# A drain between the halves of a chunk's turning, and low parts by a product with minus one, in a fused RWKV and gated-convolution kernel

## The chip, the cores and the metric

The kernel runs on one core of a Trainium2 chip. Its metric is device time in microseconds (us) of one execution. Three timed runs of the kernel before gave 322.41, 322.68 and 322.76 us; the median is 322.68 us.

## The reference, cut to what matters

All inputs are 32-bit, apart from the three weights of the second part, which are 64-bit floating point. The first part is a recurrence over 768 steps for 4 batches of 8 heads of 48 channels, the second a projection, a convolution over three neighbours in time, a gate and a projection back:

```python
for t in range(S):                       # B=4, H=8, S=768, D=48
    cur = einsum('bhd,bhe->bhde', u * k[t], v[t])
    y[:, :, t] = einsum('bhd,bhde->bhe', r[t], state + cur)
    state = w[t] * state + einsum('bhd,bhe->bhde', k[t], v[t])
x = y laid out as (B, S, H*D = 384)
h = maximum(x @ w_in, 0)                 # 384 -> 1024
c = conv_w[0] * h[t-1] + conv_w[1] * h[t] + conv_w[2] * h[t+1]
out = (h * sigmoid(c)) @ w_out           # 1024 -> 384
```

## The kernel before, in words

**Chunks.** The recurrence is cut into 24 chunks of 128 steps (4 batches of 6). For a chunk, w, k and r are loaded with time on the partitions and turned by TensorE so that channels stand on the partitions (`turns`, three banks of PSUM: w, k and r). VectorE writes zeros into four columns of w's bank (`pad`, L598), runs two scans over w (L646, L654) and multiplies k and r by them (L651, L658). The scaled keys are turned back (`kback`), scores are products of keys and r (L756, or L764 in half chunks), VectorE puts them under a mask (L796), and `within` (L848) makes the chunk's output y in one bank. The state goes from chunk to chunk through small products (L813, L878) and small vector operations.

**Turning late chunks.** The turning of chunks 0 to 7 is whole (L632, 128 by 128). From chunk 8 on (`MERGED`) it is done in two parts, f1 and f2, of 12 small transposes each (L780), in which two transposes on different halves of TensorE's rows run side by side; the keys of the chunk before are turned back in the same parts. The two halves of a row group write the same bank in f1 and in f2, with their places changed, so the end of f1 and the start of f2 must not overlap. Before, that is kept by `pad`: it waits for f1, and f2 waits for it. Between f1 and f2 the written order puts other work of TensorE.

**High and low parts.** Matrix products take numbers in a rounded 32-bit form (fp32r). A number is split into a high part and the rest, the low part, and three products (high with high, high with low, low with high) stand for one. For y, ScalarE copies the high part from the bank (L856), and VectorE subtracts it from the bank and stores the low part (L857).

**Blocks.** As soon as its chunks are there, each of 8 blocks of 384 steps runs through the second part: for each of 8 pieces of 128 hidden channels, nine products of 386 columns (L896), then ScalarE and VectorE make the gate (L908 to L917), GpSimd its low part (L918), and for each of three groups of 128 steps the products with w_out (L925); ScalarE copies the sum (L953) and SyncE stores it (L954).

**Weights.** The 64-bit weights are loaded in nine pieces and converted (L489 to L497). Six more loads of the same weights (`in_range`, L506) feed a test of their range: VectorE masks the words (L510), ScalarE sums what is out of range (L513). At the end one flag decides whether a general path must run; with these inputs it does not.

**Order.** Every operation is recorded with what it reads and writes, and then issued in the order of the list `ORDER`; `PLACES` says which bank or buffer each gets. Each engine runs its instructions in that order. A negative number in `ORDER` stands for one filler product on TensorE (L445, 256 columns), which computes nothing that is used.

Of the kernel before, what the change touches and what calls it, by code (L numbers as in the profile page):

```python
# [8 lines left out]
F32 = mybir.dt.float32  # L9
# [5 lines left out]
ALU = mybir.AluOpType  # L15
# [11 lines left out]
HALVED = 8  # L27
ORDER = [
# [135 lines left out]
]  # L164


# [155 lines left out]
def rwkv_conv_moe_kernel(  # L322
# [12 lines left out]
    nc = tc.nc  # L335
# [693 lines left out]
```

## Time and profile before

| | |
|---|---|
| median of 3 timed runs | 322.68 us |
| the profiled execution's own time | 320.73 us |
| span of the profile, first to last instruction | 318.6 us |
| TensorE's mean granted clock (1 is 2.4 GHz) | 0.999 |
| busy: TensorE, VectorE, ScalarE, GpSimd | 310.0, 260.9, 231.2, 207.3 us |
| filler products (L445) | 28 |
| small transposes of late chunks (L780) | 384 |

A profile is one execution. PE is TensorE, PEld its weight loads (which overlap PE), DVE VectorE, ACT ScalarE, POOL GpSimd, SP SyncE, which issues the DMAs. PE counts as busy from a product's start to its modelled end, and products overlap: at this share of busy time, what a product costs is read from the distance between starts, or from the chain's pieces, which follow each other end to end.

### The profile page before, as it was taken

What the parts mean: (1) busy time and instruction counts of PE and PEld (TensorE: products, weight loads), DVE (VectorE), ACT (ScalarE), POOL (GpSimd) and SP (SyncE); (2) the same over time, 40 slices, a digit from 0 to 9 for tenths busy, and PEclk for the clock granted to TensorE, in tenths of its full rate; (3) what the DMA queues carried; (4) which work ended last, traced back from release to release, by engine and by line L of the source; (5) the groups of instructions that cost most, each with busy time, mean ns of one, the idle gap of its engine ahead of it and who ended that gap; (6) DMA issues with size and microseconds to landing.
All of it is one profiled execution on the core that took longest, in us unless ns stands there. A gap on an engine that the chain in (4) does not pass through costs nothing.

```text
span 318.6 us, 11367 instructions
## 1 busy us (share of the span) xinstructions
PE 310.0 (97%) x4470; PEld 288.6 (91%) x4470; DVE 260.9 (82%) x524; ACT 231.2 (73%) x621; POOL 207.3 (65%) x283
## 2 busy tenths in 40 slices
PE   7999999999999999999999899999999999999994
PEld 4888988999898898999998899989999999999994
DVE  4999999999998799989987799868787888555350
ACT  3466889999596588887877688556787887856641
POOL 6768999999898637478289663894083394163320
PEclk9999999999999999999999999999999999999999
DMA  7999368875455457344345555474748300000005
GB/s 154 260 264 231 81 187 223 200 141 175 100 106 111 119 131 160 67 118 87 74 80 125 112 171 128 80 189 89 228 127 277 91 14 2 29 0 1 2 16 187
DMA packets 114079, 39.36 MB, mean 124 GB/s; under 512 B 102605, under 2 KB 109542, under 8 KB 114022
## 3 DMA queue, kind: packets, MB, share of 16 engines
q1 hardware_dynamic: 114020, 38.59, 49.6%
q8 instruction: 36, 0.59, 0.8%
q14 instruction: 21, 0.17, 0.2%
q10 hardware_dynamic: 2, 0.00, 0.0%
HBM read 31.88 MB, written 4.72 MB: 115 GB/s over the span
## 4 chain that ended last, share of the span: by engine, by line
PE 82%; DVE 9%; ACT 3%; issue 2%; POOL 1%; DMA 1%; SPq 1%; DVEq 0%; ACTq 0%
PE bank L925 30%; PE bank L896 27%; PE bank L848 6%; PE bank L780 5%; PE bank L764 3%; PE bank L878 3%; PE bank L756 2%; PE bank L666 2%; PE bank L632 2%; DVE bank L491 1%; DVE kr L646 1%; DVE strip L494 1%; DVE strip L912 1%; PE bank L829 1%; DVE kr L654 1%
## 5 line engine op out<-in xcount | busy, mean ns | idle before, releaser
L896 PE MATMUL bank<-xT,wi 128*128 128x386 f32 x576 | 112.7, 344 | 0.6 <-DVE strip L915 0.5
L925 PE MATMUL bank<-wo,gh 128*128 128x384 f32 x576 | 109.7, 340 | 0.0
L896 PEld LDWEIGHTS bank<-xT,wi 128*128 128x128 f32 x576 | 100.7, 188 | 2.8 <-DVE strip L915 0.8
L925 PEld LDWEIGHTS bank<-wo,gh 128*128 128x128 f32 x576 | 99.6, 188 | 1.3 <-DVE kr L654 0.2
L918 POOL TENSOR_TENSOR gh<-strip,gh 128x384 fp32r<-128x384 f32 x64 | 64.4, 1022 | 53.8 <-ACT gh L917 53.1
L910 DVE SCALAR_TENSOR_TENSOR strip<-bank,cw,strip 128x384 f32<-128x384 f32 x64 | 39.0, 610 | 15.6 <-ACT strip L909 15.2
L914 ACT ACTIVATE strip<-strip 128x384 f32<-128x384 f32 x64 | 32.6, 523 | 17.8 <-DVE strip L912 17.6
L915 DVE TENSOR_TENSOR strip<-bank,strip 128x384 f32<-128x384 f32 x64 | 34.4, 549 | 7.5 <-ACT strip L914 7.0
L684 POOL TENSOR_SCALAR_AFFINE_SELECT pm<-dg 128x1024 f32<-128x1024 f32 x24 | 26.2, 1092 | 21.2 <-PE bank L848 12.2
L912 DVE SCALAR_TENSOR_TENSOR strip<-bank,cw,strip 128x384 f32<-128x384 f32 x64 | 39.0, 612 | 1.1 <-DVE strip L910 0.3
L909 ACT ACTIVATE strip<-bank,cw 128x384 f32<-128x384 f32 x64 | 36.7, 580 | 2.0
L908 ACT ACTIVATE bank<-bank 128x386 f32<-128x386 f32 x64 | 30.1, 477 | 9.8 <-PE bank L896 9.7
L796 DVE COPY_PREDICATED pm<-upper,bank 128x512 f32<-128x512 int32 x48 | 34.1, 736 | 2.4 <-POOL pm L693 0.8
L917 ACT CAST gh<-strip 128x384 fp32r<-128x384 f32 x64 | 31.7, 512 | 5.3 <-DVE strip L915 5.0
L678 POOL TENSOR_TENSOR strip<-nat,nat 128x384 f32<-128x384 f32 x24 | 24.3, 1016 | 6.2 <-DMA nat<-in_k_dram 2.8
L693 POOL COPY pm<-kr 48x256 f32<-48x256 f32 x60 | 23.6, 395 | 6.0 <-DMA kr<-kr 3.0
L680 POOL TENSOR_TENSOR strip<-strip,ubc 128x384 f32<-128x384 f32 x24 | 24.8, 1034 | 2.7 <-issue 1.7
L646 DVE TENSOR_TENSOR_SCAN kr<-bank,one_end 128x387 f32<-128x387 f32 x24 | 23.0, 956 | 3.7 <-PE bank L780 2.6
L848 PE MATMUL bank<-pm,v 128*32 128x64 f32 (+3 forms) x1280 | 25.8, 231 | 0.0
L848 PEld LDWEIGHTS bank<-pm,v 128*32 128x32 f32 (+2 forms) x1280 | 21.8, 109 | 2.0 <-issue 1.2
L654 DVE TENSOR_TENSOR_SCAN kr<-bank,dA 128x387 f32<-128x387 f32 x24 | 23.0, 957 | 0.3
L606 ACT COPY nat<-nat 128x96 f32<-128x96 f32 x72 | 18.6, 268 | 3.5 <-DMA nat<-in_k_dram 1.9
(105 smaller groups left out, 440.6 us busy)
## 6 DMA issues: line engine op xcount, KB each, us to landing
gh<-in_moe_w_out_dram SPq DMA_DIRECT2D x5, 1152.0 KB, 6.6
nat<-in_w_dram SPq DMA_DIRECT2D x24, 192.0 KB, 3.5
nat<-in_r_dram SPq DMA_DIRECT2D x24, 192.0 KB, 3.3
nat<-in_k_dram SPq DMA_DIRECT2D x24, 192.0 KB, 3.9
gh<-in_moe_w_in_dram SPq DMA_DIRECT2D x4, 1152.0 KB
out_dram<-strip SPq DMA_DIRECT2D x24, 192.0 KB, 2.3
v<-in_v_dram SPq DMA_DIRECT2D x32, 96.0 KB, 2.7
kr<-kr SPq DMA_DIRECT2D x120, 16.1 KB, 2.4
```

The costliest lines, as they stand in the source:

```text
L796: op("DVE", "cp", lambda g=g: nc.vector.copy_predicated(out=pm.t[:, g], mask=upper.unsqueeze(1).to_broadcast([P, NP, L]), data=sc[g].t.rea ...
L848: nc.tensor.matmul(rows(a, 32)[:, ts], lhsT=lhs, rhs=rhs, start=((halved or c == 0) and i == 0), stop=(i == count - 1), skip_group_check=True)
L896: nc.tensor.matmul(t.t[:, 0:xs.stop - xs.start], lhsT=wi[:, m, a, f * P:(f + 1) * P], rhs=xT[:, x0 + m, c, xs], start=(m == 0 and j == 0), ...
L908: ("ACT", "relu", lambda: nc.scalar.activation(out=h(0, width + 2), in_=h(0, width + 2), func=AF.Relu), [t], [t]),
L909: ("ACT", "mul", lambda: nc.scalar.mul(out=a(), in_=h(1), mul=cw[:, 1, fs]), [t, "cw"], [a1]),
L910: ("DVE", "stt", lambda: nc.vector.scalar_tensor_tensor(out=a(), in0=h(0), scalar=cw[:, 0, fs], in1=a(), op0=ALU.mult, op1=ALU.add), [t], ...
L912: ("DVE", "stt", lambda: nc.vector.scalar_tensor_tensor(out=a(), in0=h(2), scalar=cw[:, 2, fs], in1=a(), op0=ALU.mult, op1=ALU.add), [t], ...
L914: ("ACT", "sig", lambda: nc.scalar.activation(out=a(), in_=a(), func=AF.Sigmoid), [], [a1]),
L915: ("DVE", "gate", lambda: nc.vector.tensor_tensor(out=g.t[:, 0:width], in0=h(1), in1=a(), op=ALU.mult), [t, a1], [g]),
L917: ("ACT", "cast", lambda: nc.scalar.copy(out=part(0)[:, 0:width], in_=g.t[:, 0:width]), [g], [key]),
L918: ("POOL", "lo", lambda: nc.gpsimd.tensor_tensor(out=part(1)[:, 0:width], in0=g.t[:, 0:width], in1=part(0)[:, 0:width].bitcast(F32), op=AL ...
L925: nc.tensor.matmul(acc.t[:, 0:DM], lhsT=part(a)[:, tt * P:(tt + 1) * P], rhs=wo[:, f, c, :], start=(f == 0 and a + c == 0), stop=(f == FT ...
```

## The change

Four things change in the code, and the order is written anew.

1. `pad` now stands before f1, which waits for it; f2 begins with a drain of TensorE, which waits until all its earlier instructions are done. There are 16 such turnings.
2. For chunks 0 to 4 (`LOWS`) the low part of y is no longer subtracted by VectorE. ScalarE once fills a 128 by 128 tile `less` with minus the identity, in a part of the tile that the last chunk writes much later; for each of these chunks three products of 128 columns add minus the high part to y's bank, and ScalarE copies the rest out.
3. Each range load also waits for the range test of the load before it.
4. `ORDER` and `PLACES` hold other numbers, and 12 fillers in place of 28.

```diff
+LOWS = 5
 ORDER = [
-    1, 3, 2, 49, 174, 173, 5, 7, 6, 8, -8, 11, 19, 14, 180, 53, 10, 13, 50, 15, 18, 20, 16, 51, 9, 177, 0, -8, -8,
...
-        op("SP", "issue", lambda: nc.sync.dma_start(out=raw.t[:, :, 0:2 * n], in_=src), [], [(raw, 0)], [raw])
+        op("SP", "issue", lambda: nc.sync.dma_start(out=raw.t[:, :, 0:2 * n], in_=src), ["seq"], [(raw, 0)], [raw])
...
-           [(raw, 0)], [raw])
+           [(raw, 0)], [raw, "seq"])
...
+    less = xT[:, 2 * KT - 1, 1, S + 1 - L:S + 1]
+    op("ACT", "fill", lambda: nc.scalar.mul(out=less, in_=ident, mul=-1.0), [], [("x", 1, NCH - 1, 1)])
...
             def one_half(second):
+                if second:
+                    nc.tensor.drain()
                 for a, c_ in (todo if not second else todo[::-1]):
...
-            op("PE", "f1", lambda: one_half(False), reads, wrote)
-            pad(nx["turned"][0], nx["turned"][0:1])
+            pad(nx["turned"][0])
+            op("PE", "f1", lambda: one_half(False), [*reads, (nx["turned"][0], 1)], wrote)
...
-        op("DVE", "kt", lambda: nc.vector.tensor_tensor(
-            out=xT[:, slots, 1, ts], in0=thirds(y.t), in1=xT[:, slots, 0, ts].bitcast(F32), op=ALU.subtract),
-            [y, ("x", odd, c, 0)], [("x", odd, c, 1)])
+        if n < LOWS:
+            def minus():
+                for m in range(KT):
+                    nc.tensor.matmul(y.t[:, m * L:(m + 1) * L], lhsT=less, rhs=xT[:, KT * odd + m, 0, ts], start=False,
+                                     stop=True, skip_group_check=True)
+            op("PE", "neg", minus, [("x", odd, c, 0), ("x", 1, NCH - 1, 1)], [y])
+            op("ACT", "xl", lambda: nc.scalar.copy(out=xT[:, slots, 1, ts], in_=thirds(y.t)), [y], [("x", odd, c, 1)])
+        else:
+            op("DVE", "xl", lambda: nc.vector.tensor_tensor(
+                out=xT[:, slots, 1, ts], in0=thirds(y.t), in1=xT[:, slots, 0, ts].bitcast(F32), op=ALU.subtract),
+                [y, ("x", odd, c, 0)], [("x", odd, c, 1)])
```

Over the whole program the instructions of each engine stay the same but for these: TensorE has 15 more products and 16 fewer fillers, and 16 drains (which the rows below leave out); VectorE 5 fewer subtractions; ScalarE 6 more copies.

**A late turning on TensorE.** Before, one turning stands so; the first two rows end f1, the last two begin f2, and `nat` holds the chunk's loaded k, r and w:

```order
L780 MATMUL bank_68<-ident,nat_133 128x64
L780 MATMUL bank_69<-ident,nat_131 128x64
L925 MATMUL bank_70<-wo,gh 128x384 x9
L780 MATMUL bank_69<-ident,nat_131 128x64
L780 MATMUL bank_68<-ident,nat_133 128x64
```

Now f2 (from the second of the two in the third row) follows f1 at once in 11 of the 16 turnings, this among them; the drain stands between the two:

```order
L783 MATMUL bank_65<-ident,nat_131 128x64
L783 MATMUL bank_68<-ident,nat_133 128x64
L783 MATMUL bank_65<-ident,nat_131 128x64 x2
L783 MATMUL bank_68<-ident,nat_133 128x64
L783 MATMUL bank_65<-ident,nat_131 128x64
```

The products with w_out that stood between the parts have moved elsewhere. Before, the small transposes stand in 32 stretches of 12; now in 11 stretches of 24 and 10 of 12. Counting full-size products (128 by 128), small transposes, and the other small products by their tile size, TensorE's order changes from one kind to another 117 times before and 93 times now; it comes back to full-size products 38 times before and 34 times now, and to the other small kinds 47 times before and 38 times now.

**Early chunks on TensorE.** Before, behind the first chunk's y (L848, in bank 67), two more chunks' transposes and a run of nine fillers follow, of which the first shows:

```order
L813 MATMUL bank_65<-v_121,kh_152 32x48 x16
L848 MATMUL bank_67<-pm_150,v_121 32x128 x16
L632 MATMUL bank_71<-ident,nat_131 128x128 x3
L703 MATMUL bank_69<-ident,kr_138 128x128 x3
L445 LDWEIGHTS ident
L445 MATMUL bank_65<-ident 128x256
```

Now the first chunk's y is in bank 71, and the new products (L865) go into it some way on, with the next chunk's y in the same bank close behind (L834 and L853 are L829 and L848 of before):

```order
L706 MATMUL bank_66<-ident,kr_139 128x128 x3
L635 MATMUL bank_64<-ident,nat_133 128x128 x3
L865 MATMUL bank_71<-xT 128x128 x3
L635 MATMUL bank_69<-ident,nat_134 128x128 x3
L818 MATMUL bank_65<-v_122,kh_153 32x48 x16
L834 MATMUL bank_71<-kr_138,sbd_146 32x128 x12
```

Of the fillers, 17 stood ahead of the first scores and 11 behind them; now 7 stand ahead and 5 behind.

**The last range loads on SyncE.** Before, stores of the output and spreads of `kr` stand between the fifth and the sixth:

```order
L506 DMA gh<-in_moe_w_out_dram 128x3x768
L675 DMA kr_138<-kr_138 16x2x129
L954 DMA out_dram<-strip_115 128x384
L506 DMA gh<-in_moe_w_out_dram 128x3x768
L582 DMA v_122<-in_v_dram 64x8x48
```

Now they stand side by side, with the last eight stores behind them:

```order
L675 DMA kr_139<-kr_139 16x2x129 x6
L967 DMA out_dram<-strip_119 128x384
L967 DMA out_dram<-strip_114 128x384
L507 DMA gh<-in_moe_w_out_dram 128x3x768 x2
L967 DMA out_dram<-strip_119 128x384
L967 DMA out_dram<-strip_120 128x384
```

The loads of v that followed have all moved ahead of them.

## Rows read from the trace of the kernel before

**Rows 1.** The page, busy us, share of the span and instructions of each engine

```profile
PE 310.0 (97%) x4470; PEld 288.6 (91%) x4470; DVE 260.9 (82%) x524; ACT 231.2 (73%) x621; POOL 207.3 (65%) x283
```

**Rows 2.** Busy time of each engine in stretches of 10 us

```profile
core 0: us, PE busy (x) PEld busy (x) DVE busy (x) ACT busy (x) POOL busy (x), PEclk, DMA share, GB/s
0.00:10.00 10.00, 7.77 (x38) 4.95 (x39) 5.26 (x18) 3.24 (x9) 7.12 (x34) 1.00 0.84 166
20.00:30.00 10.00, 9.66 (x205) 8.55 (x203) 9.66 (x24) 7.06 (x24) 8.15 (x10) 1.00 1.05 256
40.00:50.00 10.00, 9.48 (x91) 8.68 (x90) 9.97 (x25) 8.92 (x24) 9.20 (x12) 1.00 0.63 177
```

**Rows 3.** TensorE's waits over the whole span: us in total, times, longest

```profile
PE bank L780 <- issue: 0.9, 1, 0.9
PE bank L632 <- ACT nat L606: 0.8, 1, 0.8
PE bank L896 <- DVE strip L915: 0.5, 1, 0.5
PE bank L813 <- issue: 0.3, 1, 0.3
```

**Rows 4.** The chain that ended last, 98 to 137 us: start, us, what

```profile
103.66 1.93 PE bank L848 x128
...
107.89 1.06 PE bank L896 x6
108.95 0.52 PE bank L780 x12
109.47 0.73 PE bank L896 x3
...
127.45 1.03 PE bank L848 x64
```

**Rows 5.** TensorE's instructions at the end of a turning: start, us

```profile
110.42 0.22 PE L780 MATMUL bank<-ident,nat 64*128 64x64 f32 x1
...
110.48 0.22 PE L780 MATMUL bank<-ident,nat 64*128 64x64 f32 x1
...
110.64 0.62 PE L896 MATMUL bank<-xT,wi 128*128 128x386 f32 x2
```

**Rows 6.** Groups of instructions by line and shape: busy us, mean ns of one

```profile
L780 PEld LDWEIGHTS bank<-ident,nat 64*128 64x128 f32 x288 | 14.5, 138 | 2.0 <-DVE dg L681 0.3 <-issue 0.2 <-DVE xT L857 0.2
L856 ACT CAST xT<-bank 128x384 fp32r<-128x384 f32 x24 | 11.5, 480 | 5.8 <-PE bank L848 5.8
L857 DVE TENSOR_TENSOR xT<-bank,xT 128x384 fp32r<-128x384 f32 x24 | 13.0, 552 | 3.2 <-ACT xT L856 3.2
L598 DVE MEMSET bank<- 128x4 f32 x24 | 1.5, 62 | 2.3 <-PE bank L780 2.3
```

**Rows 7.** TensorE in order of time, at fillers and early transposes

```profile
6.32 1.10 PE L445 MATMUL bank<-ident 128*128 128x256 bf16 x5
8.17 0.55 PE L632 MATMUL bank<-ident,nat 128*128 128x128 f32 x3 [0.76 <-ACT nat L606]
...
12.50 0.49 PE L632 MATMUL bank<-ident,nat 128*128 128x128 f32 x3
12.83 0.49 PE L445 MATMUL bank<-ident 128*128 128x256 bf16 x3
...
19.67 1.15 PE L445 MATMUL bank<-ident 128*128 128x256 bf16 x9
20.65 1.49 PE L666 MATMUL bank<-kr,strip 128*112 128x129 f32 x12
```

**Rows 8.** VectorE's range tests (L510): duration ns, first and last start us

```profile
L510 DVE TENSOR_SCALAR gh<-gh x6: 683/752/1219, 140.2 to 269.8; 128x1152 int32<-128x1152 int32 x5, 128x768 int32<-128x768 int32 x1
```

**Rows 9.** The range loads (L506), from issue to landing

```profile
DMA to landing us min/median/max: 5.5/6.6/6.7
```

More of the change, by code (lines that the diff above doesn't have):

```diff
@@ L668, in stage_a @@
             op("PE", "gather", gather, [kr, (kr, 1), sel], [gt])
-            op("ACT", "kh", lambda: nc.scalar.copy(
+            op("ACT", "gk", lambda: nc.scalar.copy(
                 out=planes(KT)[0:R], in_=gt.t[0:R, 0:2 * SL].rearrange("p (a w) -> p a w", a=2)),
```

263 rows, old and new, of tables (ORDER, PLACES) are left out of this document.

## The prediction

> **What bounds the kernel now.** I read four views in this order: the page's busy times, the stretches of 10 us, TensorE's waits, and the chain of waits with single starts. The reader is to see first that TensorE is busy for 310.0 of 318.6 us [rows 1]. The stretches then show that this isn't TensorE alone: from 20 to 30 us VectorE is busy for 9.66 of 10 us and from 40 to 50 us for 9.97, beside TensorE's 9.66 and 9.48, with ScalarE at 7.06 and 8.92 [rows 2]. So it matters who waits for whom, and the waits answer it: past the first 10 us TensorE has one wait of 0.5 us for the gate's VectorE work, and two of 0.9 and 0.3 us that no semaphore explains [rows 3]. TensorE therefore never stands still for long; its own instructions set the time, and the edit has to be counted in TensorE's time. VectorE's relief counts only where TensorE waits for it.
>
> Since products overlap, I take prices from the chain's pieces and from starts. Six full-size products take 1.06 us, 0.177 each, and three between two stretches of turning take 0.73 in place of 0.53: a stay in full-size products has a fixed price of 0.20. A pair of small transposes follows the last after 0.06 us (110.42 to 110.48), so six pairs would be 0.36; twelve transposes take 0.52, so a stretch of turning has a fixed price of 0.16. For the other small products, 128 take 1.93 and 64 take 1.03; twice 1.03 less 1.93 leaves 0.13 [rows 4, 5]. All three are what TensorE pays for changing its tile size: the first product of the new size starts 0.16 us behind the last pair of transposes, in place of 0.06 [rows 5]. The Trainium skill says it so too (TensorEngine Tiling, Key Properties: a change of tiling mode, not of the tile alone, drains the engine); by that rule a drain written out should cost little where the tile size changes anyway, and about as much as such a change elsewhere.
>
> **Fewer changes of tile size.** By the order shown, stretches of turning go from 32 to 21, stays in full-size products from 38 to 34, in other small ones from 47 to 38. The saving is 11 x 0.16 + 4 x 0.20 + 9 x 0.13 = 1.76 + 0.80 + 1.17 = 3.7 us. The products that stood between the parts aren't gone, only moved next to others of their kind.
>
> **The drains.** No row shows one between instructions of one tile size. From below: in a change of tile size the array empties and the next start comes after 0.16 in place of 0.06, which leaves 0.10 for a drain; less than nothing is excluded, since a drain removes no work. For the five that have other work between f1 and f2 even that may be paid already, so 11 x 0.10 = 1.1 us is the lower end. From above: the drain waits until the last transpose has ended (0.22 us by its row), and only then is the next weight load sent (0.138 us); 0.22 + 0.14 - 0.06 = 0.30, for all 16 4.8 us [rows 5, 6]. The nearest row is the stretch's own price, which has an emptied array and a start from nothing in it: 0.16, for all 16 2.6 us. I take that.
>
> The Trainium skill has a rule against the edit (TensorE: Matmul & The Clock Gate, Single matmul latency): a product by itself at the full clock takes (398 + columns) / 2.4 ns, 192 ns for 64 columns, which a stream hides and a drain shows. An estimate by that page is 0.19 - 0.06 = 0.13 per drain, 2.1 us for 16, and the sum below would be 0.5 us lower. The trace has 0.22 for such a transpose, so it puts the price higher, and I stay with the row.
>
> **pad.** It takes 62 ns and moves out of the middle: VectorE waited 2.3 us in all for f1 before it could write [rows 6], and has time to spare there. Now f1 waits for it, and behind f1 all of TensorE is queued. It needs only a free bank, which f1 needs as well, and is written on VectorE behind the bank's last readers. I cost it at nothing; what hides it is TensorE's work ahead of f1. Without that cover it would cost a VectorE instruction ahead of it, about 0.5 us, per turning.
>
> **Low parts.** Removed are 5 subtractions of 0.552 us, 2.8 us of VectorE; added are 5 copies on ScalarE at 0.48 as for the high part, 2.4 us [rows 6], in stretches where ScalarE still has 1 to 3 of 10 us [rows 2]. On TensorE 15 products of 128 columns with a full weight load are added. The transposes of 128 columns in the early chunks are nearest: three of them start at 12.50 and the next product at 12.83, 0.11 each [rows 7]. That is 15 x 0.11 = 1.65 us, all on the path. Between the zero of a product hidden in a wait and 0.18 for a full one, 0 to 2.7.
>
> **Fillers.** A filler takes 0.11 (nine from 19.67 to 20.65). The ten fewer ahead of the first scores stand in front of waits for ScalarE's and VectorE's first results (0.76 us behind five of them [rows 7]), so nothing is saved there: the wait gets longer by the filler. Behind them there are 11 - 5 = 6 fewer, 0.65 us, saved if what they bridged is there in time.
>
> **The wait for the gate.** With 2.8 us less on VectorE, the one wait of TensorE for it, 0.5 us between 40 and 50 us [rows 2, 3], goes; what would be late next is ScalarE's share of the same gate.
>
> **Range loads.** SyncE now stops at the sixth load until the fifth has landed (6.6 us [rows 9]) and VectorE has tested it (0.75 us); behind it wait the last eight stores. Their work is at the end of the last blocks. Before, the last test began at 269.8 [rows 8], with some 48 us of the span to go; a wait of 7 us or so is hidden by the blocks' work. Without that cover, strips wouldn't come free and up to 7 us would show. I cost it at nothing.
>
> **Sum.** -3.7 + 2.6 + 1.65 - 0.65 - 0.5 = -0.6 us. The profiled execution takes 320.73, 318.6 of it span, so it would go to 320.1; the timed runs' median lies 1.95 above it, so I forecast 322.68 - 0.6 = 322.1 us.
>
> **Rivals.**
> - *A drain shows the whole latency.* Place: the start of f2; price 0.30 x 16 = 4.8 in place of 2.6, so +2.2: 324.3 us, slower. It decides from the point where one drain costs 0.20, where the sum is nil. For it speaks that a drain stops the queue, in which weight loads run ahead; against it, that a change of tile size has an empty array too and costs 0.16.
> - *The early chunks shorten.* If VectorE sets the pace of the first 50 us, 2.8 us less of it lets TensorE's real work start sooner than its fillers and waits allow. TensorE has 28 x 0.11 = 3.1 us of fillers, 0.65 of which is in the sum, and little to wait for; at best some 2 us more come: 320.1 us. VectorE's 9.97 of 10 us speaks for it, TensorE's short waits against it.
> - *The new order takes it back.* Each place where the written order has TensorE close behind another engine can wait: the first chunk's high part, its copy, the product and the copy of the rest go through ScalarE twice, and the next y in that bank comes close behind the product, after three transposes and sixteen small products. One such wait of 0.6 us makes it 322.7: no change.
> - *The clock.* It was at 1.00, 2.4 GHz, over the first 10 us, with waits among fillers [rows 2, 7]. The Trainium skill (TensorE: Matmul & The Clock Gate, Why this matters for your kernels) says that idle gaps send it back to the lower level. If with ten fillers fewer it fell to 1.2 GHz there, some 3 us of products would take 6: 325 us.
>
> **How the numbers follow.** About 0.65 us, 0.2%, is what a measurement of this kernel can tell from none. Chances: forecast 0.40 (321.1 to 323.1 by itself), whole latency 0.22, early chunks 0.15, taken back 0.18, clock 0.05. The forecast lies at the edge of what can be told: 0.25 of its 0.40 fall faster, 0.13 within, 0.02 slower. Early chunks give 0.15 faster; taken back 0.02 faster, 0.11 within, 0.05 slower; whole latency 0.03 within, 0.19 slower; clock 0.05 slower. That is 0.42 faster, 0.27 same, 0.31 slower. The range runs from the early chunks' case with a little more, 319.6, to the whole latency's with another short wait, 324.8.
>
> **What would show it.** In the changed profile: a turning of 24 in one piece of the chain, twelve pairs and one fixed price, 0.88 us, and the drain on top: 1.04 us if it costs 0.16, 1.18 if 0.30; full-size products between small ones seldom as threes of 0.73; the 15 new products in threes of 0.33; no wait for the gate between 40 and 50 us; SyncE's sixth load about 8 us behind the fifth and no wait of ScalarE's for a strip. The prediction is wrong if TensorE's waits add up to over 2 us past the first 15, if the granted clock is below 1.00 in the first 20 us, or if the turnings in one piece are longer than 1.1 us.

## The result, and the profile after

The changed kernel takes 326.13 us (median of 20 runs, 323.23 to 330.12) against 322.94 for the kernel before (20 runs). Some executions are disturbed, at a lower mean clock and several us longer: the medians hold them, the ratios of one kernel to another leave them out. The ratio is 1.0076 with a 95% interval of [1.0052, 1.0100], 2.5 us slower. The forecast was 322.1, in a range of 319.6 to 324.8, with faster as the likeliest. The profiled execution takes 326.62 us, 324.9 of it span, against 320.73 and 318.6. So profile stands against profile with 5.9 us, the runs' middles with 2.5 to 3.2: the profile of before is one of the best executions of that kernel (the lowest of its 20 runs took 320.97 us).

The page's busy times, as in [rows 1], and the first stretch of 10 us, as in [rows 2]; TensorE is first, then its weight loads, VectorE, ScalarE, GpSimd, the granted clock, DMA's share and GB/s:

```profile
PE 311.9 (96%) x4469; PEld 291.2 (90%) x4469; DVE 259.3 (80%) x519; ACT 233.1 (72%) x627; POOL 206.5 (64%) x283
```

```profile
0.00:10.00 10.00, 8.12 (x32) 5.09 (x32) 5.14 (x17) 3.60 (x10) 7.26 (x35) 1.00 0.83 164
```

The 5.9 us aren't to be found here: TensorE is busy for 1.9 us more and VectorE for 1.6 less. TensorE's waits, as in [rows 3], say more (us in total, times, longest):

```profile
PE bank L853 <- issue: 1.4, 1, 1.4
PE bank L891 <- DMA v<-in_v_dram: 1.4, 1, 1.4
PE bank L374 <- DVE table L378: 1.2, 1, 1.2
PE bank L891 <- ACT strip L966: 1.0, 1, 1.0
PE bank L669 <- DVE dA L653: 0.7, 1, 0.7
PE bank L783 <- issue: 0.6, 1, 0.6
```

The wait for the gate's VectorE work (0.5 us) has gone. Two of at least 1 us stand in its place: for a load of v near 128 us, and for ScalarE's copies of output rows near 214 us. Past 15 us they and the stops without a reason (`issue`) add up to over 4 us; the prediction named 2 as its limit. The stops without a reason are 2.2 us here and 1.2 in the kernel before [rows 3]; the largest lies at 200.8 us, in the middle of one line's products, and what makes them stays open.

The drains are in the chain that ended last (start, us, what). First a turning in one piece, 24 transposes with the drain in the middle; then one whose parts have 32 small products between them. To compare: twelve transposes were 0.52 us in [rows 4].

```profile
197.28 0.52 PE bank L783 x11
197.80 0.09 issue
197.89 0.59 PE bank L783 x12
198.48 0.90 PE bank L853 x50
```

```profile
136.70 0.52 PE bank L783 x8
137.21 0.61 PE bank L891 x32
137.82 0.14 issue
137.96 0.59 PE bank L783 x12
```

The one piece takes 1.20 us where the prediction had 1.04 for a drain of 0.16 and 1.18 for one of 0.30: 0.32 per drain. Apart, the drain's own stop is 0.14 us and the second part 0.07 longer: 0.21. The others agree: by single starts, the gap at the drain is 0.30 to 0.31 us in all 11 joined turnings, against 0.06 between pairs, and 0.35 to 0.36 in four of the five others, against 0.15; in the fifth the drain costs 0.11.

The start, as in [rows 7] (start, us, engine, line, tile, count, and what it waited for); two rows of the kernel before come first, then the changed kernel's:

```profile
9.76 1.49 PE L666 MATMUL bank<-kr,strip 128*112 128x129 f32 x12
...
13.25 1.16 PE L756 MATMUL bank<-kr 48*128 48x128 f32 x16
```

```profile
7.67 0.90 PE L706 MATMUL bank<-ident,kr 128*128 128x128 f32 x3 [0.36 <-DVE kr L654]
8.36 1.49 PE L635 MATMUL bank<-ident,nat 128*128 128x128 f32 x6
10.59 2.89 PE L669 MATMUL bank<-kr,strip 128*112 128x129 f32 x12 [0.74 <-DVE dA L653]
13.27 0.85 PE L635 MATMUL bank<-ident,nat 128*128 128x128 f32 x3
...
15.45 0.82 PE L759 MATMUL bank<-kr 48*128 48x128 f32 x9
```

Read L669 against L666: twelve products of 129 columns take 2.89 us here and 1.49 there. Three transposes take 0.85 at 13.27, and 0.55 from 8.17 in the kernel before. By the starts of single products, 128 columns are mostly 213 to 214 ns apart until 14.8 us here; in the kernel before they are so until 8 us and 109 ns from there on. That is TensorE's lower and its higher level, 1.2 and 2.4 GHz, though the stretch's row has 1.00; in e4 below the same 214 ns stand beside a granted clock of 0.50. The first scores (L759) start at 15.45 us, 2.2 later than before (L756).

The groups of [rows 6], and of the new copies (busy us, mean ns of one, idle time before them):

```profile
L783 PEld LDWEIGHTS bank<-ident,nat 64*128 64x128 f32 x288 | 14.4, 138 | 4.5 <-issue 4.5
L870 DVE TENSOR_TENSOR xT<-bank,xT 128x384 fp32r<-128x384 f32 x19 | 10.4, 551 | 6.4 <-ACT xT L861 6.3
L868 ACT CAST xT<-bank 128x384 fp32r<-128x384 f32 x5 | 2.4, 485 | 0.5 <-PE bank L865 0.5
```

They are as counted: 2.6 us off VectorE by this row and that of [rows 6] (10.4 against 13.0; 2.8 were forecast), 2.4 on ScalarE. The drains show in the weight loads: 4.5 us of waiting for nothing but the queue, where it was 0.3 and less.

One of the four changes never reached the chip. The tie between the range loads, `"seq"`, is a name that restricts the written order alone; no instruction waits for it. The last two loads go out 2.0 us apart, the second of them 7 us ahead of the first one's test:

```profile
269.42 2.40 SPq L507 DMA_DIRECT2D gh<-in_moe_w_out_dram  x2
```

```profile
278.37 0.75 DVE L511 TENSOR_SCALAR gh<-gh 128x1152 int32<-128x1152 int32 x1
```

### The profile page after: what moved, and what is told of

It reads as the page before. It is cut to its first block, busy times and chain, and to the rows that moved or that the text cites. A ratio compares the mean times of both kernels' runs of the same rounds, so it can differ in the third digit from the quotient of the medians.

```text
span 324.9 us, 11373 instructions
## 1 busy us (share of the span) xinstructions
PE 311.9 (96%) x4469; PEld 291.2 (90%) x4469; DVE 259.3 (80%) x519; ACT 233.1 (72%) x627; POOL 206.5 (64%) x283
## 4 chain that ended last, share of the span: by engine, by line
PE 85%; DVE 5%; SPq 3%; DMA 3%; issue 3%; ACT 1%; DVEq 0%; ACTq 0%
PE bank L938 30%; PE bank L909 27%; PE bank L853 6%; PE bank L783 4%; PE bank L635 3%; PE bank L891 3%; PE bank L759 2%; PE bank L767 2%; PE bank L669 2%; SPq L577 1%; PE bank L834 1%; SPq L678 1%; DMA v<-in_v_dram 1%; PE bank L818 1%; DMA nat<-in_k_dram 1%
## 5 line engine op out<-in xcount | busy, mean ns | idle before, releaser
L923 DVE SCALAR_TENSOR_TENSOR strip<-bank,cw,strip 128x384 f32<-128x384 f32 x64 | 38.5, 609 | 13.6 <-ACT strip L922 13.5
L928 DVE TENSOR_TENSOR strip<-bank,strip 128x384 f32<-128x384 f32 x64 | 34.1, 550 | 12.5 <-ACT strip L927 12.0
L925 DVE SCALAR_TENSOR_TENSOR strip<-bank,cw,strip 128x384 f32<-128x384 f32 x64 | 38.4, 609 | 0.8
L853 PE MATMUL bank<-pm,v 128*32 128x64 f32 (+3 forms) x1280 | 25.7, 231 | 1.4 <-issue 1.4
L853 PEld LDWEIGHTS bank<-pm,v 128*32 128x32 f32 (+2 forms) x1280 | 22.0, 109 | 3.4 <-issue 2.0
```

The source lines that it names most:

```text
L853: nc.tensor.matmul(rows(a, 32)[:, ts], lhsT=lhs, rhs=rhs, start=((halved or c == 0) and i == 0), stop=(i == count - 1), skip_group_check=True)
L923: ("DVE", "stt", lambda: nc.vector.scalar_tensor_tensor(out=a(), in0=h(0), scalar=cw[:, 0, fs], in1=a(), op0=ALU.mult, op1=ALU.add), [t], ...
L925: ("DVE", "stt", lambda: nc.vector.scalar_tensor_tensor(out=a(), in0=h(2), scalar=cw[:, 2, fs], in1=a(), op0=ALU.mult, op1=ALU.add), [t], ...
L928: ("DVE", "gate", lambda: nc.vector.tensor_tensor(out=g.t[:, 0:width], in0=h(1), in1=a(), op=ALU.mult), [t, a1], [g]),
```

## The experiments

Each time is the median, with the ratio to the kernel before measured in the same batch; the changed kernel's own is 1.0076. Where two experiments are compared, the difference is that of their ratios (1% is 3.2 us), with the two intervals taken together behind ±.

**1. The drain by itself: the kernel before with a drain ahead of every second part (e1).**

```diff
             def one_half(second):
+                if second:
+                    nc.tensor.drain()
                 for a, c_ in (todo if not second else todo[::-1]):
```

> The kernel before with a drain at the start of each f2 and nothing else changed; the order and the pads stay. Theory (a drain shows a product's whole latency): in the changed kernel's trace a drain behind other small products makes the gap to the first transpose 0.354 us in place of 0.150, so 16 x 0.2 = 3.2 us slower than before (2 to 4.5), and single gaps of 0.35 or more ahead of each f2. Rival (a drain costs what a change of tile size costs, and the changed kernel lost its time by its order): the tile size changes ahead of nearly every f2 here, so nothing to 1 us.

325.95 us, 1.0067 [1.0038, 1.0097]: 2.2 us slower. The chain has the drain as in the changed kernel's parts that stand apart:

```profile
142.70 1.16 PE bank L850 x64
143.87 0.14 issue
144.00 0.59 PE bank L780 x12
```

Rows like these would make 16 x 0.21 = 3.4 us. By the starts of all 16, against those of the kernel before, the gap grows by 0.20 to 0.23 in ten places, behind small products, by 0.13 to 0.15 in five, four of them behind full-size ones, and by 0.37 in one: 3.2 us in all. By the runs it is 2.2 [1.2, 3.1], 0.14 each. Where other work stands ahead of it, the drain costs about what the prediction took, 0.16.

**2. Joined parts in the kernel before's order (e2):** pad ahead of f1, f2 behind f1 at all 16 places, drained.

```diff
+            pad(nx["turned"][0])
-            op("PE", "f1", lambda: one_half(False), reads, wrote)
-            pad(nx["turned"][0], nx["turned"][0:1])
+            op("PE", "f1", lambda: one_half(False), [*reads, (nx["turned"][0], 1)], wrote)
```

> The kernel before with pad ahead of f1, f2 moved up right behind f1 in all 16 turnings, and the drain between them. Theory: each turning saves a stretch's price (0.16) and what the work between lost by its own change of tile size (0.13 to 0.20), 4.6 to 5.8 us in all, and pays 0.30 for the drain, 4.8 us: within 1 us of before. Rival (a drain costs 0.16 or less): 2 to 4 us faster than before.

329.53 us, 1.0202 [1.0140, 1.0265]: a miss. I had put pad right ahead of f1, and TensorE waited for it in the middle of f1:

```profile
PE bank L776 <- DVE bank L594: 2.9, 5, 0.9
```

So pad is free only when written well ahead, as the changed order does (no such row above). Here it isn't, and the run says nothing more of the joining.

**3. The changed kernel with pad between the parts, and no drain (e3).**

```diff
-                if second:
-                    nc.tensor.drain()
...
-            pad(nx["turned"][0])
-            op("PE", "f1", lambda: one_half(False), [*reads, (nx["turned"][0], 1)], wrote)
+            op("PE", "f1", lambda: one_half(False), reads, wrote)
+            pad(nx["turned"][0], nx["turned"][0:1])
```

> The changed kernel in its own order, but without drains: pad stands right behind f1 and f2 waits for it, as before. Theory: f2 right behind f1 now waits for f1's last product, VectorE's turn and pad's 0.06 us, which is longer than a drain's 0.30; 0 to 4 us slower than the changed kernel, and gaps of over 0.4 us in the 11 joined turnings. Rival (the drain is what costs, a semaphore would be cheaper): 2 to 4 us faster than the changed kernel.

330.76 us, 1.0223 [1.0178, 1.0267], 4.7 ± 1.6 us above the changed kernel. The wait for pad takes the drain's place:

```profile
PE bank L779 <- DVE bank L597: 6.2, 14, 1.0
```

With parts joined, a drain is the cheaper order of the two.

**4. The changed kernel without the products: VectorE subtracts (e4).**

```diff
-LOWS = 5
+LOWS = 0
```

> The changed kernel with the low parts of chunks 0 to 4 subtracted by VectorE at the place where ScalarE's copy stood; no products with minus one, and minus the identity isn't made. Theory (the 15 products are all on the path): they took 1.84 us of TensorE, so 1 to 1.8 us faster than the changed kernel. Rival (VectorE sets the pace early and the products fill waits): the same or up to 2 us slower than the changed kernel.

329.40 us, 1.0192 [1.0139, 1.0245]: 3.7 ± 1.9 us slower than the changed kernel. TensorE, whose list of waits between 15 and 60 us is empty in the changed kernel, now has some there (first fence); and the granted clock falls at the start (second: stretches of 2 us, columns as above).

```profile
PE bank L753 <- DVE xT L864: 1.0, 1, 1.0
...
PE bank L812 <- DVE pm L795: 0.5, 1, 0.5
PE bank L629 <- DVE pm L795: 0.5, 1, 0.5
```

```profile
10.00:12.00 2.00, 1.54 (x9) 1.57 (x10) 2.00 (x6) 0.94 (x5) 1.92 (x3) 0.70 1.03 203
12.00:14.00 2.00, 2.00 (x11) 1.82 (x11) 0.37 (x4) 0.89 (x4) 1.92 (x4) 0.50 0.97 190
```

The fall isn't what e4 loses by: its first scores start at 14.91 us, 0.5 ahead of the changed kernel's; the same products lie 0.1 ahead at 25 us, 1.4 behind at 35 and 2.8 at 70. In the new order the products pay for themselves, and the loss isn't theirs. The kernel before with them alone (e7) was to show it in the old order:

> The kernel before with only one part of the change: the low parts of five chunks' outputs by a product with minus one on TensorE and a copy on ScalarE, in place of VectorE's subtraction; nothing else. Theory (the prediction's own): TensorE bounds the kernel, so 15 products cost their 1.8 us and little comes back: 324.2 to 325.5. Rival (the opposite experiment on the changed kernel cost 3 us): VectorE sets the pace of the first 50 us, the 2.8 us taken off it come back on TensorE's path, and the time is 321 to 323.5, within 0.6 us of the kernel before or below it.

334.08 us, 1.0348 [1.0310, 1.0385]. Both theories fall, and the run doesn't decide between them: where I had put ScalarE's new copies, VectorE waited 3.3 us for one of them and TensorE 2.2 us behind it, and TensorE waited 1.6 us for a copy of the high part. A further wait of 2.3 us, at 257 us, lies far behind these copies and isn't explained. What the products cost in the old order stays open.

**5. Fillers.** Seen in the starts of products, the low clock was the next suspect. e5 has ten more fillers in the changed kernel, four ahead of operation 28 (the first products behind the three fillers), six ahead of 22 (L669's first); e6 is the kernel before with 12 of its 28, e11 with 22 (six fewer behind the first scores).

```diff
-    -1, -1, -1, 28, ... 186, 22,
+    -1, -1, -1, -1, -1, -1, -1, 28, ... 186, -4, -4, -4, -4, -4, -4, 22,
```

> The changed kernel with ten more fillers ahead of its first scores: four behind its first three, ahead of the masks' transposes, and six ahead of the first state products, where its trace shows TensorE idle for 0.6 and 0.95 us. Theory (low clock): the changed kernel's products of 128 columns are 213 to 214 ns apart from 3.9 to 14.6 us, those of the kernel before only until 8 us and 109 from there, because idle stretches with few fillers in them hold TensorE at its lower level, 1.2 GHz. With the fillers the spacing falls to 109 ns by 10 us at the latest, the first scores start at 13.2 to 14.0 us instead of 15.45, and the time falls by 1.5 to 2.2 us, to about 324. Rival (order): the first scores are late because VectorE takes the second chunk's first scan too early; the spacing may fall, but the scores stay at 15.2 us or later and the time within 0.6 us of the changed kernel's 326.1.

> The kernel before with 12 of its 28 fillers (7 ahead of the first scores, 5 behind), order kept otherwise. Theory (low clock): TensorE stays at 213 ns per 128 columns past 8.2 us, until 12 us or longer; the first scores start at 14.2 to 15.5 us instead of 13.25 and the kernel takes 1 to 2.2 us longer. Rival of the prediction (fillers stand in front of waits and cost or give nothing ahead of the first scores, 0.11 us each behind): first scores at 13.2 to 13.4 us, time 0 to 0.7 us less.

> The kernel before with all 17 fillers ahead of the first scores, and 5 of the 11 behind. Theory (the ones ahead hold the clock up, the ones behind cost 0.11 us each): first scores at 13.25 us as before, six fewer behind give 0.65 us, and against the run with 7 ahead (first scores at 14.24) it gains what late scores cost, up to 1.0: 321.0 to 322.2. Rival (late scores are made up for later, since the first 100 us have slack against loads and VectorE): 322.0 as the run with 7 ahead, or more.

e5: 324.49 us, 1.0042 [1.0005, 1.0079], 1.1 ± 1.4 below the changed kernel. The spacing falls to 110 ns at 8.8 us, but the six fillers wait 1.6 us for their bank, and the scores start at 14.56. e6: 322.01, 0.9970 [0.9945, 0.9996]. Its clock stays low until 12.5 us, as the theory says, and the scores are 1 us late:

```profile
10.15 2.63 PE L661 MATMUL bank<-kr,strip 128*112 128x129 f32 x12
...
14.24 0.94 PE L751 MATMUL bank<-kr 48*128 48x128 f32 x12
```

Yet the time is no longer but 1 us shorter. Along the program, the same products lie 1.0 us behind the kernel before's until 30 us and 0.4 to 0.6 from there to 100: the six fewer fillers behind the scores take back what the start lost. e11, with these six gone alone: 322.15, 0.9963 [0.9940, 0.9986], 1.2 us faster. The prediction's 0.65 for them is right or small; what a late start costs the old order can't be told from nothing (e6 against e11: 0.2 ± 1.1 us). In e11's trace, with all 17 fillers ahead as in the kernel before, the spacing falls only at 10.3 us and the scores start at 13.92, not at the 13.25 that was expected.

**6. The start of the new order.** e9 puts two more fillers ahead of 28 and eight ahead of 22, these into another bank; e13 has none there and only the four ahead of 28.

> The changed kernel with ten more fillers ahead of its first scores, as in the run with ten fillers before, but two ahead of the masks' transposes and eight ahead of the first state products, and these eight into a PSUM bank that nobody holds (in the run before they waited 1.6 us for VectorE to have read theirs). Theory (idle stretches hold TensorE at its lower level, and a late clock costs the start): spacing of 128 columns 109 ns from 9 us on, first scores at 13.2 to 13.9 us instead of 14.56 (15.45 in the changed kernel), time 323.4 to 324.1. Rival: what comes earlier than 14.56 waits for VectorE or a load later; the time stays at the 324.5 of the run before or above.

> The changed kernel with four more fillers ahead of the masks' transposes near 7 us, and none in the later stretch, where both runs with fillers made TensorE wait 1.6 and 2.5 us for their bank. Theory (the start is late because TensorE's clock comes late, and what is late there is late at the end): 128 columns at 109 ns from 8.7 us on, as with ten fillers in the first such run; the first state products start near 10.5 us, the first scores at 13.2 to 13.6 us in place of 15.45, and the time is 323.0 to 323.8. Rival (the stretch of about 1.2 us without work before the first state products takes the clock down again, as 2.9 us did): 213 ns from about 10.7 us, first scores at 14.5 to 15.5, time 324.5 to 325.5.

e9: 329.13, 1.0164 [1.0127, 1.0202], a miss that shows the mechanism from the other side. The eight wait 2.5 us for VectorE to have written their bank. The products ahead of that wait are 213 ns apart, the eight behind it 109, and those behind them slow down again, with 110 ns for the first and 214 from the third:

```profile
12.32 1.03 PE L442 MATMUL bank<-ident 128*128 128x256 bf16 x8 [2.48 <-DVE bank L597]
13.19 2.66 PE L665 MATMUL bank<-kr,strip 128*112 128x129 f32 x12
```

e13: 324.11, 0.9983 [0.9951, 1.0015]: 2.0 us below the changed kernel by the medians, 3.0 ± 1.3 by the ratios. The clock is up from 9.2 us, L669's twelve start at 10.67 and take 1.4 us to the next start, the scores start at 13.46. The 2.0 us won by 15 us are still there at 125 us (2.2); in this execution 0.3 are left at 140, which experiment 8 explains. Theory right in mechanism and size of the start; the median is 0.3 above its range.

**7. ScalarE's queue near 212 us.** In the changed kernel (start, us):

```profile
210.29 0.29 ACT L609 COPY nat<-nat 128x96 f32<-128x96 f32 x1
214.16 0.27 ACT L609 COPY nat<-nat 128x96 f32<-128x96 f32 x1 [3.57 <-DMA nat<-in_r_dram]
214.33 0.52 ACT L927 ACTIVATE strip<-strip 128x384 f32<-128x384 f32 x1
214.76 0.46 ACT L966 COPY strip<-bank 128x384 f32<-128x384 f32 x1
```

ScalarE stands 3.57 us for a load, and the output copies (L966) that free TensorE's bank stand behind it. Operation 1770, that second copy of raw rows, goes behind them: e10 with e9's fillers, e14 with e13's, e15 by itself.

```diff
-    1770, ... 1121, 1768, 1111,
+    ... 1121, 1768, 1111, 1770,
```

> The kernel with ten fillers in a free bank, and one more edit: on ScalarE one copy of a late chunk's raw rows, which waits 3.4 to 3.6 us for its load near 212 us, goes behind two copies of output rows that stand behind it. Theory (the new order has waits of its own): TensorE's wait of 0.8 to 1.2 us for those rows' copies, which every run of the changed order so far has, goes, and the time falls by 0.8 to 1.0 us against the run without this edit. Rival: the copy is then late for the next turning and the wait only moves; within 0.3 us of the run without it.

> The kernel with four more fillers, and ScalarE's copy of raw rows near 212 us behind the two copies of output rows that follow it. Theory: TensorE's wait of 0.8 to 1.2 us for those rows goes; against the run without this edit the time falls by 0.5 to 1.1 us. Rival (another release is late in its place): within 0.3 us of it, or above.

> The changed kernel with ScalarE's copy of raw rows near 212 us moved behind the two copies of output rows, and no more fillers: the other half of the run that had both. Theory (two separate losses, which add up): 1.0 to 1.5 us below the changed kernel's 326.1, so 324.6 to 325.1, TensorE's wait for the output rows' copies gone, first scores at 15.4 us as there; with the fillers' share of about 2 us that adds up to what both gave (4.2 us). Rival (the late start hides it, or the wait only shows when the start is early): within 0.5 us of 326.1.

e10: 330.49, 1.0197 [1.0146, 1.0247], no gain that the runs could show over e9; its bank was 3.3 us late at the start. e14: 321.94, 0.9977 [0.9951, 1.0003]; its median is 2.2 below e13's, but by the ratios it is 0.2 ± 1.3, no difference that the runs show. e15: 325.26, 1.0030 [0.9991, 1.0069], 1.5 ± 1.5 below the changed kernel. In the traces of all three the products past 215 us come 1.2 to 1.3 us earlier against those at 205 than in the changed kernel's, and the row for L966 has gone. So the rows show the wait and its end; that it adds up with the start's 3.0 us in time is not shown (e14 against the changed kernel: 3.2 ± 1.1). The start in e14 has its longest wait ahead of L665, and the clock stays up behind it:

```profile
10.61 1.55 PE L665 MATMUL bank<-kr,strip 128*112 128x129 f32 x12 [1.60 <-DVE dA L649]
```

**8. The load of v (e16).** In the changed kernel SyncE's queue stands full from 118 to 134 us, and v is under way from 126.85:

```profile
126.85 3.17 DMA v<-in_v_dram
130.02 0.14 issue
130.15 0.57 PE bank L891 x13
```

The wait can cost more than its own length. In e13's and e15's profiles, where it is 1.7 and 2.5 us, the granted clock falls behind it; e13's stretches of 2 us, columns as above:

```profile
128.00:130.00 2.00, 1.67 (x49) 1.58 (x49) 1.96 (x5) 1.49 (x6) 1.19 (x2) 0.67 0.97 190
130.00:132.00 2.00, 2.00 (x7) 2.00 (x7) 1.92 (x5) 1.94 (x7) 1.95 (x3) 0.50 0.28 60
```

The 24 products with w_out behind it, in the changed kernel's profile first and then in e15's:

```profile
131.30 4.36 PE bank L938 x24
```

```profile
133.50 6.43 PE bank L934 x24
```

From the wait's end to the end of these 24 it is 5.5 us in the changed kernel's profile, 7.0 in e13's, 8.4 in e15's. With the longer waits that is 1.9 us of e13's lead gone, and 4.0 us lost by e15, between 125 and 140 us.

e16 is e14 with both halves of that load (944, 945) ahead of the other loads and copies that stood before them.

```diff
-    1199, 1143, ... 1141, ... 1197, 944, ... 945,
+    944, 945, 1199, 1143, ... 1141, ... 1197,
```

> The kernel with four more fillers and ScalarE's copy moved, and the two loads of v that TensorE waits for near 128 us ahead of three loads and copies that stand before them in SyncE's queue (some 3.5 us earlier there). Theory (the third of the new order's own waits: SyncE's queue stands back to back from 118 to 134 us and the load is issued only 0.4 to 2 us before TensorE needs it): the wait of 1.4 us for v goes and the time falls from 321.9 to 320.4 to 321.0. Rival (what is put behind v is late in its place): 321.5 to 323.

321.55 us, 0.9918 [0.9890, 0.9947], 2.6 us faster than the kernel before, 5.1 ± 1.2 below the changed kernel and 1.9 ± 1.2 below e14 (0.4 by the medians, which were taken in different batches). TensorE's waits have no v any more:

```profile
PE bank L665 <- DVE dA L649: 1.6, 1, 1.6
PE bank L370 <- DVE table L374: 1.2, 1, 1.2
```

The median is above the expected 321.0, the ratio better than that. The clock's fall behind this wait is one way in which runs of the changed kernel can spread over 7 us; how often it comes is not shown.

**9. Two drains in a row (e12), and the range loads untied (e8).**

```diff
                 if second:
                     nc.tensor.drain()
+                    nc.tensor.drain()
```

```diff
-in_=src), ["seq"], [(raw, 0)], [raw])
+in_=src), [], [(raw, 0)], [raw])
```

> The changed kernel with two drains in a row where it has one. Theory (a drain's price is the emptying of the array, which the second finds done): 0 to 0.5 us over the changed kernel's 326.1, gaps of 0.31 us in the joined turnings stay below 0.35. Rival (each drain has a price of its own): gaps grow by 0.06 to 0.25 us each, time 1 to 4 us over it.

> The changed kernel without the tie that sends its range loads singly: each may start as soon as its buffer is free. Theory (range loads cost nothing): within 0.6 us of the changed kernel's 326.1, and the one wait of 1.4 us for v at 128 us stays. Rival (the tie holds SyncE's queue up, and with it the loads behind): the wait for v shrinks below 0.5 us and the time falls by 0.8 to 1.5 us.

e12: 326.89, 1.0126 [1.0081, 1.0171], 1.6 ± 1.6 us above the changed kernel. The stop grows from 0.09 to 0.17 us:

```profile
112.17 0.17 issue
112.34 0.59 PE bank L783 x12
```

By the gap the rival is right, at the low end of its range: 0.39 us in the joined turnings in place of 0.31. A second drain costs 0.08, 1.3 us for 16; if the first one's own price is the same, some 0.24 of its 0.32 is the emptying. e8: 326.33, 1.0095 [1.0056, 1.0134]. Its trace has the same instructions as the changed kernel's, in the same order on SyncE: since nothing waits for the tie, taking it out changes nothing, and e8 is the changed kernel once more. It says nothing of what a real tie would cost. It does show how far one and the same program's ratio moves from batch to batch, 0.2%, and that its waits for no reason differ (1.0 us in place of 1.4 at the largest).

## Why the prediction was wrong

- **The step that failed first: fillers.** "Nothing is saved there" was right, nothing lost was not. With the ten fillers the clock came up at 8 us, without them at 14.8, in the middle of the work that the first scores wait for: +2.0 us by e13's rows, 3.0 ± 1.3 by its ratio. The fillers aren't all that decides it: four more profiles with the changed kernel's start have the rise at 15 to 16 us (e3, e8, e12, e15), but e4, with the same seven fillers ahead, was up at 7.7 us, and e11, with the 17 of the kernel before, only at 10.3. I had this as a rival (the clock) at 0.05, with 325 us, and had it as a fall; it is a rise that doesn't come. The row that I leaned on had 1.00 for the first 10 us, and could not have told: the changed kernel's has 1.00 too. The durations in [rows 7] could: five fillers take 1.10 us at 6.32, nine take 1.15 at 19.67. I read only the nine. The Trainium skill (TensorE: Matmul & The Clock Gate, Why this matters for your kernels), which says that idle gaps send the clock to its lower level, had the direction; e10 agrees, with 109 ns ahead of 3.5 us between two starts and 213 behind them.
- **Drains: mis-sized.** Predicted 16 x 0.16 = 2.6 us; the rows have 11 x 0.32 + 5 x 0.21 = 4.6 (4.5, since one of the five costs 0.11). The nearest row held for drains that stand behind other work, as e1 shows (0.14 by the runs, 0.20 by the starts), but in a joined turning it is about the 0.30 that the prediction had worked out as its upper end. So joining wins 0.16, and at best the 0.13 to 0.20 of the work that stood between, and pays 0.32. The rival for this had 0.30 and +2.2; its chance should have been the larger for the eleven joined ones. The estimate by the Trainium skill's formula (TensorE: Matmul & The Clock Gate, Single matmul latency), 0.13, is less than either row.
- **The new order takes it back: mis-sized.** One wait of 0.6 us was foreseen, behind the product with minus one. None came there. Two others did, of 1.0 us (ScalarE behind a load; by the rows of e14 and e15, in time not clear of noise) and 1.4 (v; e16, 1.9 ± 1.2 in time, which may hold falls of the clock behind the wait).
- **Low parts: the size right, the reading short.** The 15 products take 1.84 us of TensorE's starts against 1.65. But e4 shows VectorE's relief to be worth more than that in this order (3.7 ± 1.9 us net of the products). Whether it would be in the old one is open.
- **Right:** six later fillers (e11), and pad at nothing. The gate's wait went as forecast, but not shown for the reason given: e4, where VectorE has its five subtractions back, has no such wait either.
- **Range loads: right at nothing, by luck.** The stop that was to be hidden doesn't exist: no instruction carries the tie, and the sixth load goes out 2.0 us behind the fifth, not 8.
- **Fewer changes of tile size:** the part on turnings, 0.16 each, agrees with 1.20 - 0.32 = 0.88 us for 24. The other 2.0 us I could not read apart from the waits; no run tries them alone.

The sum, profile against profile: -0.6, and drains +2.0, products +0.2, start +2.0, ScalarE +1.0, v +1.4 make +6.0 us; the profiles differ by 5.9. It leaves the unread 2.0 us as predicted, so it bears them out only as far as the other terms are right, and the match is in part luck: the stops without a reason, 1.0 us more than before, aren't in it, and the runs' middles differ by 2.5 us, so that the rest of the 5.9 is where these two executions lie among their kernels' runs. Of the miss, 4.4 us by the rows are three places in the order, 5.1 ± 1.2 by the ratios; with these mended (e16) the rest of the change is worth 2.6 us on the good side, of which the six later fillers alone gave 1.2 (e11).

## What to carry to other kernels

Where products that only keep TensorE busy are taken out of a start, compare the durations of the same products at either end of it: the level of the clock is in them, and a late clock moves everything that hangs on the start. A drain cost 0.13 to 0.23 us behind other work and 0.32 between two streams of one tile size; count these apart. In a new order, look first for an instruction that waits for a load with another engine's release queued behind it, on ScalarE as on SyncE. And see in the trace that an edit reached the chip: a dependence that only orders the list makes no engine wait.

## What the runs showed of the hardware

- TensorE ran at half speed (213 to 214 ns for 128 columns) over 3.9 to 14.8 us while the granted clock's rows had 1.00; in e4, where the spacing had been 109 ns from 8.2 us and then fell back, they had 0.70 and 0.50.
- Behind 3.5 us between two starts (e10) it slowed from 109 to 213 ns from the second product on, behind 1.6 us (e4) from the fourth product on; behind 1.2 (e13) and 1.9 us (e14) it didn't. In e9, where it was at 213 ns ahead of 2.9 us between two starts, it was at 109 behind them and slowed from the third product of L665 on. Near 128 us the granted clock fell to 0.50 behind waits for v of 1.7 (e13) and 2.5 us (e15), and stayed at 1.00 behind 1.4 (the changed kernel, e14) and 2.5 us (e9).
- A drain behind a drain costs 0.08 us, the first one 0.32 between streams of one tile size, 0.20 to 0.23 behind other small products, and 0.15 behind full-size ones (e1).
- With pad between two joined parts the second starts 0.43 us behind the last transpose at best (e3); with a drain 0.31.
